# Attention weights left undivided: one reciprocal per visit, spread through DRAM and multiplied into the product with v

## The chip, the cores and the metric

One Trainium2 chip, one of its cores. The metric is the device time of one execution in microseconds (us). The engines are TensorE (PE in the profile; PEld is its loading of weights), VectorE (DVE), ScalarE (ACT), GpSimd (POOL) and SyncE (SP), which here issues every DMA. Each engine works through its own instructions in a fixed order and waits at an instruction whose inputs are not there.

## The reference

Attention with a threshold, then an expert layer. Batch 8, 8 heads, 576 queries and keys, 64 dimensions a head, inner width 2048, all in float32 (the expert weights arrive as float64).

```python
def _attn_ref(q, k, v, tau):
    scale = 1.0 / np.sqrt(q.shape[-1])
    scores = scale * np.matmul(q, k.transpose(0, 1, 3, 2))
    thresh = np.max(scores, axis=-1, keepdims=True) - tau
    scores = np.where(scores >= thresh, scores, -1000000000.0)
    scores = scores - np.max(scores, axis=-1, keepdims=True)
    attn = np.exp(scores)
    attn = attn / (np.sum(attn, axis=-1, keepdims=True) + 1e-09)
    return np.matmul(attn, v).astype(np.float32)

def _moe_ref(x, w_in, w_out):          # x: attention's output, [4608, 512]
    h = x @ w_in
    g = h * (1.0 / (1.0 + np.exp(-h)))
    return (g @ w_out).astype(np.float32)
```

## The kernel before

**Precision.** Products that need float32 run as several cheaper ones: a number is split into a high half (rounded) and a low half (the rest), and the product of the two low halves is left out. q and k are split for the scores, the attention weights w and v for the product with v, and its result x, the expert weights and the activation g for the experts.

**Visits and tiles.** A visit is a pair of heads (`VISITS`, L44). Batch 0 goes through four visits "low" and four "high"; "low" works in plain float32 (`direct`). The seven other batches have four visits "all" each: nine tiles of 128 queries by 576 keys, five of the first head (the fifth holds the last 64 queries of both heads) and four of the second. That is 288 tiles, 272 of them not direct. A tile's path:

- `scores` (L406): four matmuls, into one of two PSUM buffers s
- `soft1`: DVE takes the negated maximum (L416) and from it the threshold (L419)
- `soft1b`: ACT takes the exponential into w (L426), one of four buffers; its bias is the negated maximum
- `soft2`: DVE zeroes what is below the threshold and sums each row (L435), which frees s; then adds 1e-9 (L439) and takes the reciprocal (L443)
- `soft2b`: ACT scales w by that reciprocal (L448)
- `soft3`: the high half of w is rounded, by ACT in the first 36 slots (L457) and by POOL after them (L459); POOL subtracts for the low half in two pieces, 512 and 64 columns wide (L462, L465); a transposing DMA (L475) puts the halves, hl (three buffers), into wT (three buffers, one per head)

The hl row has nine blocks of 128: the high half takes four and a half of them, and the low half's last 64 columns lie in the fifth beside it, so that both meet the same rows of v there.

**Product with v.** `av` (L490) runs some tiles after a visit's last one: 14 steps for each of the two heads into the one PSUM bank a. `av_post` (L508, L509) writes x as two f16 halves, by ACT and DVE. `load_v`, `vmax`, `vscale` and `split_v` prepare v per batch; `vscale` holds a reduction across partitions on POOL (L113).

**Experts.** `h_unit` (L524) and its tanh, product and split (L532, L533, L541, L547), and `o_unit` (L562) with the store (L571, L573), are queued as units once a half batch of x is there, and laid between the tiles at a planned rate. After the last tile only such units are left.

**Order.** The text of the program is written slot by slot (L693 on), one tile per slot, with what is due in each (`at`) and priorities for scores and softmax. A scheduler with a model of the machine then fixes the order on each engine. SP's queue holds all the DMAs in one order.

## Time and profile before

| | |
|---|---|
| times of the three runs | 1360.35, 1365.4, 1726.3 us; median 1365.4 |
| profiled execution | 1360.35 us, span 1360.4 us |
| mean granted TensorE clock | 0.950 |
| PE busy | 1183.7 us, 87% of the span |
| DVE busy | 1002.8 us, 74% |
| ACT busy | 817.5 us, 60% |
| POOL busy | 789.9 us, 58% |
| DMA | 158.15 MB, mean 116 GB/s |

The span runs from the first to the last instruction of the profiled execution, which is also its time. A busy share is a mean over stages with different limits: until about 200 us the expert weights are decoded beside the first visits, up to about 1190 us attention and experts run together, and the rest is experts alone. Matmuls are pipelined, so a busy PE is not PE at its peak; the profile shows a mean of 287 ns for a matmul of L524, while 1312 matmuls end in the last 160 us, one per 122 ns. In the rows below, "x<-y" are a group's output and inputs by the names above, "xN" its count, then busy us, mean ns, and the idle time of the engine just before it with what ended it.

### The profile page before, as it was taken

What the parts mean: (1) busy time and instruction counts of PE and PEld (TensorE: products, weight loads), DVE (VectorE), ACT (ScalarE), POOL (GpSimd) and SP (SyncE); (2) the same over time, 40 slices, a digit from 0 to 9 for tenths busy, and PEclk for the clock granted to TensorE, in tenths of its full rate; (3) what the DMA queues carried; (4) which work ended last, traced back from release to release, by engine and by line L of the source; (5) the groups of instructions that cost most, each with busy time, mean ns of one, the idle gap of its engine ahead of it and who ended that gap; (6) DMA issues with size and microseconds to landing.
All of it is one profiled execution on the core that took longest, in us unless ns stands there. A gap on an engine that the chain in (4) does not pass through costs nothing.

```text
span 1360.4 us, 26858 instructions
## 1 busy us (share of the span) xinstructions
PE 1183.7 (87%) x9392; PEld 899.9 (66%) x9392; DVE 1002.8 (74%) x2619; ACT 817.5 (60%) x1493; POOL 789.9 (58%) x964
## 2 busy tenths in 40 slices
PE   3774787898599979898899969899799999999998
PEld 2453555666477757676677757677577777777777
DVE  4987997897598967968497856869478787872421
ACT  3776775675476756656375745757367666662432
POOL 2647984787478656754476646556467666661000
PEclk9887888999799999999899979999799999999999
DMA  6454955778467656664475556565466565543000
GB/s 226 140 185 125 197 129 94 146 139 170 88 133 155 122 106 129 131 128 86 99 132 124 118 96 136 101 127 121 82 122 116 115 129 115 106 88 53 6 19 18
DMA packets 363479, 158.15 MB, mean 116 GB/s; under 512 B 329552, under 2 KB 338256, under 8 KB 363344
## 3 DMA queue, kind: packets, MB, share of 16 engines
q1 hardware_dynamic: 363344, 156.43, 55.5%
q8 instruction: 74, 1.21, 0.4%
q14 instruction: 61, 0.50, 0.1%
HBM read 66.72 MB, written 9.44 MB: 56 GB/s over the span
## 4 chain that ended last, share of the span: by engine, by line
DVE 35%; PE 34%; issue 13%; ACT 6%; POOL 6%; DMA 5%; SPq 2%; POOLq 0%; ACTq 0%; DVEq 0%
PE o L562 15%; PE h L524 8%; DVE w L435 8%; DVE sm L416 6%; DVE gbuf L547 6%; PE s L406 5%; PE a L490 5%; DVE qstack L310 3%; DVE th L533 3%; DMA vraw<-in_vL 2%; DMA wT<-hl 2%; ACT w L426 2%; POOL hl L459 2%; POOL hl L462 2%; ACT w L448 2%
## 5 line engine op out<-in xcount | busy, mean ns | idle before, releaser
L524 PE MATMUL h<-x,wst 128*128 128x288 f16 (+2 forms) x3072 | 422.3, 290 | 22.6 <-DVE th L533 19.1
L562 PE MATMUL o<-gbuf,wst 128*128 128x288 f16 (+2 forms) x3072 | 419.4, 293 | 22.4 <-DVE gbuf L547 16.1
L562 PEld LDWEIGHTS <-wst 128*128 128x128 f16 x3072 | 296.4, 100 | 117.1 <-issue 27.1
L459 POOL TENSOR_SCALAR hl<-w 128x576 f16<-128x576 f32 x264 | 187.3, 710 | 317.9 <-ACT w L448 69.1
L524 PEld LDWEIGHTS <-wst 128*128 128x128 f16 x3072 | 290.7, 99 | 119.2 <-issue 37.5
L462 POOL TENSOR_TENSOR hl<-w,hl 128x512 f16<-128x512 f32 x272 | 332.0, 1220 | 28.0 <-issue 13.9
L426 ACT ACTIVATE w<-s,sm 128x576 f32<-128x576 f32 x288 | 211.0, 736 | 204.5 <-POOL hl L465 135.4
L435 DVE SCALAR_TENSOR_TENSOR w<-s,sm,w 128x576 f32<-128x576 f32 x288 | 232.6, 810 | 110.4 <-ACT w L426 108.7
L448 ACT ACTIVATE w<-w,sm 128x576 f32<-128x576 f32 x288 | 218.2, 770 | 86.5 <-DVE sm L443 81.6
L416 DVE TENSOR_REDUCE sm<-s 128x1 f32<-128x576 f32 x288 | 215.1, 748 | 44.4 <-PE s L406 42.3
L406 PE MATMUL s<-khi,qstack 128*128 128x288 f32 x608 | 160.4, 346 | 70.0 <-DVE w L435 36.9
L547 DVE SCALAR_TENSOR_TENSOR gbuf<-th,gbuf 128x288 f16<-128x288 f32 (+2 forms) x256 | 167.3, 656 | 20.9 <-ACT gbuf L541 20.2
L406 PEld LDWEIGHTS s<-khi,qstack 128*128 128x128 f32 x608 | 98.5, 198 | 98.8 <-issue 71.4
L490 PE MATMUL a<-wT,v 128*64 128x288 f16 (+1 forms) x1680 | 142.4, 294 | 16.1 <-DMA wT<-hl 15.0
L532 ACT ACTIVATE th<-h,msc 128x288 f32<-128x288 f32 (+2 forms) x256 | 126.3, 495 | 49.5 <-DVE gbuf L547 30.0
L541 ACT ACTIVATE gbuf<-th 128x288 f16<-128x288 f32 (+2 forms) x252 | 109.9, 438 | 44.5 <-DVE th L533 43.9
L406 PE MATMUL s<-klo,qstack 128*128 128x288 f32 x608 | 134.2, 304 | 0.0
L533 DVE SCALAR_TENSOR_TENSOR th<-th,h 128x288 f32<-128x288 f32 (+2 forms) x256 | 113.2, 444 | 27.6 <-ACT th L532 25.4
L490 PEld LDWEIGHTS <-v 128*64 128x64 f16 x1680 | 91.3, 110 | 56.7 <-issue 41.9
L465 POOL TENSOR_TENSOR hl<-w,hl 128x64 f16<-128x64 f32 x272 | 115.3, 424 | 0.0
L406 PEld LDWEIGHTS s<-klo,qstack 128*128 128x128 f32 x608 | 102.2, 197 | 0.0
L320 POOL TENSOR_TENSOR klo<-kraw,khi 128x576 fp32r<-128x576 f32 x64 | 95.6, 1493 | 1.4 <-ACT khi L318 1.3
(82 smaller groups left out, 868.8 us busy)
## 6 DMA issues: line engine op xcount, KB each, us to landing
qraw<-in_qT SPq DMA_DIRECT2D x128, 144.0 KB, 3.0
kraw<-in_kT SPq DMA_DIRECT2D x128, 144.0 KB, 3.0
vraw<-in_vL SPq DMA_DIRECT2D x32, 320.0 KB, 3.5
wraw<-in_w_out SPq DMA_DIRECT2D x16, 512.0 KB, 4.0
out_t<-ot SPq DMA_DIRECT2D x56, 144.0 KB, 2.0
wT<-hl SPq DMA_TRANSPOSE x304, 3.3
gbuf<-in_w_in SPq DMA_DIRECT2D x8, 512.0 KB, 5.1
wraw<-in_w_in SPq DMA_DIRECT2D x8, 512.0 KB, 4.9
```

Of the source, the lines that this page charges most:

```text
L406: nc.tensor.matmul(s_ps[:, j, :HALF], lhs, kk[:, j * HALF : (j + 1) * HALF], start=(n == 0), stop=(n == len(seq) - 1),)
L416: nc.vector.tensor_reduce(out=negm, in_=s_ps[:, :, :HALF], op=ALU.max, axis=AX.XY, negate=True)
L426: nc.scalar.activation(wtile[t].rearrange("p (j c) -> p j c", j=2), sps[t][:, :, :HALF], AF.Exp, bias=small[t][:, 0:1],)
L435: nc.vector.scalar_tensor_tensor(out=w3, in0=s_ps[:, :, :HALF], scalar=sm[:, 1:2], in1=w3, op0=ALU.is_ge, op1=ALU.mult, accum_out=sm[:, 2:3],)
L448: nc.scalar.activation(w, w, AF.Copy, scale=r)
L459: nc.gpsimd.tensor_scalar(out=fl[:, 0:S], in0=w, scalar1=1.0, scalar2=1.0, op0=ALU.mult, op1=ALU.mult)
L462: nc.gpsimd.tensor_tensor(out=fl[:, 640:1152], in0=w[:, 0:512], in1=fl[:, 0:512], op=ALU.subtract)
L490: nc.tensor.matmul(a_ps[odd * D : (odd + 1) * D, :n], vt[:, lo_v, odd, kv, :], wT[v, b * H + 2 * p + odd][:, kw, c0 - base : c0 - base + n ...
L524: nc.tensor.matmul(ph[:, :n], wi(c, f, lo_w), x16[b, lo_x][:, c, c0 : c0 + n], start=(k == 0), stop=(k == 11),)
L533: nc.vector.scalar_tensor_tensor(out=th[:, :n], in0=th[:, :n], scalar=1.0, in1=ph[:, :n], op0=ALU.add, op1=ALU.mult,)
L547: nc.vector.scalar_tensor_tensor(out=g[:, 1, :n], in0=th[:, :n], scalar=2.0**-14, in1=g[:, 0, :n], op0=ALU.mult, op1=ALU.subtract,)
L562: nc.tensor.matmul(ps[:, :n], wo(f, d, lo_w), g[:, lo_g, :n], start=(f == 0 and k == 0), stop=(f == NF - 1 and k == 2),)
```

## The change

The weights w are no longer divided by their sum. For every tile that is not direct:

- the threshold moves from DVE to POOL, and POOL also makes a bias for the exponential: the negated maximum plus 5 ln 2, so that w is 32 times larger and its halves keep enough bits undivided
- the sum of each row goes into one column of a visit's tile `sums`; L439, L443 and L448 fall away
- the high half is always ACT's; the low half is one subtraction of 576 columns on POOL, right behind the high one in hl
- once per visit, `spread_sums` takes one reciprocal of all tiles' sums (up to nine columns), writes it to DRAM as one row, and reads it back by three DMAs as `rows`, spread over the partitions of each head's columns
- `av_post` multiplies the product with v by `rows` on DVE into a float32 tile; ACT rounds its high half, POOL subtracts for the low one

The low half of w now begins in the middle of a block, so v's high half must be there in a second arrangement: `split_v` makes nine blocks, the last four by two DMAs within SBUF. The host puts v's first 64 rows where the doubled last 64 stood; the direct visits read the last 64 from `vlast`. To make room, w has three buffers instead of four, raw v four instead of five (so v is loaded twice from batch 1 on: once for its maximum, once to be split), and th, o and the new x share four buffers. The dates of v's work and of batch 0's splits move.

```diff
 def split_v(b, p):
-    o = sb.tile([P, 2, 2, 5, D], F16, tag="v16", name=f"v16_{b}_{p}", bufs=4)
-    nc.scalar.activation(o[:, 0], t, AF.Copy, scale=s)
+    hi = sb.tile([P, 2, 9, D], F16, tag="vhi", name=f"vhi_{b}_{p}", bufs=3)
+    lo = sb.tile([P, 2, 5, D], F16, tag="vlo", name=f"vlo_{b}_{p}", bufs=3)
+    nc.scalar.activation(hi[:, :, 0:5, :], t, AF.Copy, scale=s)
...
+    nc.sync.dma_start(out=hi[0:D, :, 5:9, :], in_=hi[D:P, :, 0:4, :])
+    nc.sync.dma_start(out=hi[D:P, :, 5:9, :], in_=hi[0:D, :, 1:5, :])
 def soft1(t):
-    w = sb.tile([P, S], F32, tag="w32", name=f"w32_{t}", bufs=4)
+    w = sb.tile([P, S], F32, tag="w32", name=f"w32_{t}", bufs=3)
...
-        nc.vector.tensor_scalar(
+        if tiles[t][0] not in direct:
+            nc.gpsimd.tensor_scalar(
+                out=sm[:, 5:6], in0=negm, scalar1=LIFT * math.log(2.0), scalar2=1.0,
+                op0=ALU.add, op1=ALU.mult,
+            )
+        (nc.vector if tiles[t][0] in direct else nc.gpsimd).tensor_scalar(
             out=thr, in0=negm, scalar1=-1.0, scalar2=ntau, op0=ALU.mult, op1=ALU.add
 def soft2(t):
+    total = sums[v][:, t - first_tile[v] : t - first_tile[v] + 1]
         op0=ALU.is_ge, op1=ALU.mult, accum_out=total,
+    if v not in direct:
+        small.pop(t)
+        return
+def spread_sums(v):
...
+    nc.vector.tensor_scalar(
+        out=r[:, :n], in0=sm[:, :n], scalar1=1e-9 * 2.0**LIFT, scalar2=None, op0=ALU.add
+    )
+    nc.vector.reciprocal(out=r[:, :n], in_=r[:, :n])
+    d = dram.tile([9 * P], F32, tag="rs", name=f"rs_{v}", bufs=4)
+    nc.sync.dma_start(out=d[: n * P].rearrange("(j p) -> p j", p=P), in_=r[:, :n])
+    R = sb.tile([P, S], F32, tag="rows", name=f"rows_{v}", bufs=2)
+    nc.sync.dma_start(out=R[0:D, :cols], in_=d[0:cols].partition_broadcast(D))
+    nc.sync.dma_start(
+        out=R[D:P, cols - D : cols], in_=d[cols : cols + D].partition_broadcast(D)
+    )
+    nc.sync.dma_start(
+        out=R[D:P, : cols - D], in_=d[cols + D : 2 * cols].partition_broadcast(D)
+    )
 def soft3(t):
-    if t < EARLY:
-        nc.scalar.activation(fl[:, 0:S], w, AF.Copy)
-    else:
-        nc.gpsimd.tensor_scalar(
-            out=fl[:, 0:S], in0=w, scalar1=1.0, scalar2=1.0, op0=ALU.mult, op1=ALU.mult
-        )
-    nc.gpsimd.tensor_tensor(
-        out=fl[:, 640:1152], in0=w[:, 0:512], in1=fl[:, 0:512], op=ALU.subtract
-    )
-    nc.gpsimd.tensor_tensor(
-        out=fl[:, 576:640], in0=w[:, 512:576], in1=fl[:, 512:576], op=ALU.subtract
-    )
+    nc.scalar.activation(fl[:, 0:S], w, AF.Copy)
+    nc.gpsimd.tensor_tensor(out=fl[:, S : 2 * S], in0=w, in1=fl[:, 0:S], op=ALU.subtract)
 def av(v, p, c0, n):
-    steps = [(0, k, k if k < 5 else k - 5) for k in range(9)] + [(1, k, k) for k in range(5)]
+    steps = [(vhi, k) for k in range(9)] + [(vlo, k) for k in range(5)]
 def av_post(v, p, c0, n, a_ps):
+    x = sb.tile([P, WID], F32, tag="th", name=f"x32_{v}_{c0}", bufs=4)
+    nc.vector.tensor_tensor(
+        out=x[:, :n], in0=a_ps[:, :n], in1=rows[v][:, c0 - base : c0 - base + n], op=ALU.mult
+    )
+    nc.scalar.activation(hi, x[:, :n], AF.Copy)
+    nc.gpsimd.tensor_tensor(out=lo, in0=x[:, :n], in1=hi, op=ALU.subtract)
 # schedule
+            if p == 0:
+                at(-2, load_vlast)
...
+        at(last_b + 1, lambda v=v: spread_sums(v))
...
-                at(V_SLOT + p, lambda p=p: split_v(0, p))
+                at(first_high + 5 * p - 2, lambda p=p: split_v(0, p))
...
-                at(u + 9 * p - 40, lambda b=b, p=p: load_v(b, p))
-                at(u + 9 * p - 34, lambda b=b, p=p: vmax(b, p))
-                at(u + 9 * p + 4, lambda b=b, p=p: split_v(b, p))
+                at(u + 6 * p - 36, lambda b=b, p=p: load_v(b, p))
+                at(u + 6 * p - 30, lambda b=b, p=p: vmax(b, p))
+                at(u + 9 * p - 2, lambda b=b, p=p: load_v(b, p))
+                at(u + 9 * p + 3, lambda b=b, p=p: split_v(b, p))
```

More of the change, by code (lines that the diff above doesn't have):

```diff
@@ L217, in wo, with load_vlast @@
         return w16[:, 4 * NK + f, o : o + P]
+    vlast = sb.tile([P, H, D], F32, tag="rows", name="vlast", bufs=2)
+    def load_vlast():
+        nc.sync.dma_start(out=vlast[D:P], in_=vL[0, 0:D, :, 4, :])
     vmx = {}
@@ L225, in load_v @@
     def load_v(b, p):
-        t = sb.tile([P, 2, 5, D], F32, tag="vraw", name=f"vraw_{b}_{p}", bufs=5)
+        t = sb.tile([P, 2, 5, D], F32, tag="vraw", name=f"vraw_{b}_{p}", bufs=4)
         nc.sync.dma_start(out=t, in_=vL[b, :, 2 * p : 2 * p + 2])
@@ L381, in attention_moe @@
     small = {}
+    sums = {}
+    rows = {}
+    first_tile = {}
     wT = {}
@@ L427, in soft1b @@
             wtile[t].rearrange("p (j c) -> p j c", j=2), sps[t][:, :, :HALF], AF.Exp,
-            bias=small[t][:, 0:1],
+            bias=small[t][:, 0:1] if tiles[t][0] in direct else small[t][:, 5:6],
         )
@@ L443, in soft2 @@
         nc.vector.reciprocal(out=sm[:, 4:5], in_=sm[:, 3:4])
+    def spread_sums(v):
+        kind = visits[v][2]
+        ta, tb, ranges = VISITS[kind]
+        n = len(ta) + len(tb)
+        cols = sum(c for _, c in ranges)
+        sm = sums.pop(v)
+        r = sb.tile([P, 9], F32, tag="rsum", name=f"rsum_{v}", bufs=2)
+        nc.vector.tensor_scalar(
[12 more added lines that the diff above has]
+        )
+        rows[v] = R
     def soft2b(t):
+        if tiles[t][0] not in direct:
+            return
         w = wtile[t]
@@ L502, in new_x16, with av_post @@
             x16[b, r] = xp[b % 2].tile([P, NK, S], F16, tag=f"x16_{r}", name=f"x16_{b}_{r}")
[L504 removed]
+    def av_post(v, p, c0, n, a_ps):
+        b = visits[v][0]
         if (b, 0) not in x16:
```

48 lines of the change are left out of this document (28 added, 20 removed).

## The prediction

> **What bounds the kernel now.** I read first how busy TensorE is by stage, then what it waits for, then what holds the engine that it waits for. The table by windows of the profile before has one row per stage (start:end, length, then busy us and instructions of PE, PEld, DVE, ACT and POOL, the granted clock, the DMA share, GB/s):
>
> ```profile
> 0.00:200.00 200.00, 127.41 (x761) 87.33 (x761) 168.44 (x397) 131.74 (x242) 130.91 (x138) 0.85 0.62 167
> 200.00:400.00 200.00, 163.64 (x1250) 121.87 (x1250) 159.23 (x427) 126.35 (x217) 136.98 (x171) 0.91 0.66 128
> 400.00:1000.00 600.00, 539.23 (x4410) 415.20 (x4410) 452.59 (x1219) 363.87 (x660) 364.25 (x461) 0.97 0.60 118
> 1000.00:1200.00 200.00, 196.75 (x1666) 152.25 (x1665) 164.42 (x441) 134.87 (x249) 134.32 (x165) 1.00 0.59 114
> 1200.00:1360.00 160.00, 156.62 (x1312) 123.21 (x1310) 58.12 (x138) 60.71 (x127) 23.40 (x33) 1.00 0.19 36
> sum 1360.00, PE 1183.66 PEld 899.87 DVE 1002.81 ACT 817.53 POOL 789.86; mean PE 236.73 PEld 179.97 DVE 200.56 ACT 163.51 POOL 157.97
> ```
>
> PE's work does not change, so only its idle time and its clock can. It idles 72.6 us of the first 200, 36.4 of the next 200, 60.8 of the 600 after them and 6.6 in the rest: 176 us. The clock is low exactly where PE idles (0.85, 0.91) and 1.00 where it doesn't, so idle time that goes also brings a little clock back. The second view is what PE waited for (total us, times, longest):
>
> ```profile
> PE s L406 <- DVE w L435: 36.9, 26, 10.6
> PE h L524 <- DVE th L533: 19.1, 20, 2.8
> PE o L562 <- DVE gbuf L547: 16.1, 6, 5.0
> PE a L490 <- DMA wT<-hl: 15.0, 5, 8.8
> ...
> POOL hl L459 <- issue: 67.5, 8, 11.1
> POOL v_all L113 <- issue: 43.9, 7, 7.5
> ```
>
> Most waits name DVE, but the last two rows point further back. Once per batch POOL runs a reduction across partitions (L113, for the scale of v), and around it POOL stands still for no visible reason. The timeline of batch 6 (start, length, idle before in brackets) shows what that does:
>
> ```profile
> 792.61 0.67 POOL L459 TENSOR_SCALAR hl<-w 128x576 f16<-128x576 f32 x1 [0.60 <-DMA wT<-hl]
> 799.61 0.38 POOL L113 PARTITION_ALL_REDUCE v_all<-v_one  x1 [6.33 <-issue]
> 807.15 1.14 POOL L462 TENSOR_TENSOR hl<-w,hl 128x512 f16<-128x512 f32 x1 [7.17 <-issue]
> ...
> 808.60 0.74 ACT L426 ACTIVATE w<-s,sm 128x576 f32<-128x576 f32 x1 [14.36 <-POOL hl L465]
> ...
> 803.06 0.82 PE L406 MATMUL s<-khi,qstack 128*128 128x288 f32 x2 [6.09 <-DVE sm L419]
> 810.35 0.82 PE L406 MATMUL s<-khi,qstack 128*128 128x288 f32 x2 [5.00 <-DVE sm L443]
> ...
> 220.40 0.50 PE L406 MATMUL s<-khi,qstack 128*128 128x288 f32 x2 [0.48 <-DVE v_sc L131]
> 968.58 0.82 PE L406 MATMUL s<-khi,qstack 128*128 128x288 f32 x2 [4.30 <-DVE sm L443]
> ```
>
> POOL is away from 793.3 to 807.2. DVE waits for the reduction's result in the first half, the exponentials wait in the second for POOL to free a buffer of weights, and PE idles 11.1 us. Such PE rows stand at six places after 200 us, 15 rows from 220.40 to 968.58, 54 us together. So of the 100.4 us idle between 200 and 1200, 54 belong to this pause and 46 are small waits, mostly for DVE.
>
> **The change, priced.** Rows by line and shape (us busy in all, mean ns):
>
> ```profile
> L419 DVE TENSOR_SCALAR sm<-sm,ntau 128x1 f32<-128x1 f32 x288 | 59.0, 207 | 2.8
> L439 DVE TENSOR_SCALAR sm<-sm 128x1 f32<-128x1 f32 x288 | 41.4, 145 | 1.2
> L443 DVE RECIPROCAL sm<-sm 128x1 f32<-128x1 f32 x288 | 44.2, 156 | 2.5
> L448 ACT ACTIVATE w<-w,sm 128x576 f32<-128x576 f32 x288 | 218.2, 770 | 86.5 <-DVE sm L443 81.6 <-DVE v_sc L131 4.3
> L457 ACT ACTIVATE hl<-w 128x576 f16<-128x576 f32 x8 | 5.4, 674 | 0.0
> L459 POOL TENSOR_SCALAR hl<-w 128x576 f16<-128x576 f32 x264 | 187.3, 710 | 317.9 <-ACT w L448 69.1 <-issue 67.5 <-DMA wT<-hl 58.7
> L462 POOL TENSOR_TENSOR hl<-w,hl 128x512 f16<-128x512 f32 x272 | 332.0, 1220 | 28.0 <-issue 13.9
> L465 POOL TENSOR_TENSOR hl<-w,hl 128x64 f16<-128x64 f32 x272 | 115.3, 424 | 0.0
> L543 POOL TENSOR_SCALAR gbuf<-th 128x256 f16<-128x256 f32 x4 | 1.7, 434 | 1.3 <-DVE th L533 1.0
> L768 POOL MEMSET const-float32-1.0<- 128x1 f32 x1 | 0.1, 99 | 0.0
> L509 DVE SCALAR_TENSOR_TENSOR x<-a,x 128x288 f16<-128x288 f32 x56 | 25.2, 449 | 43.9 <-ACT x L508 43.8
> ```
>
> DVE: 272 of the 288 tiles lose the threshold, the addition and the reciprocal, 272 x (207+145+156) = 138 us. The 32 visits gain an addition and a reciprocal of up to nine columns, 32 x 0.30 = 10 us by the same rows. The product with the spread reciprocals takes the place of L509 at about its 449 ns. Net -128 us.
>
> ACT: the scaling of the weights (770) goes and the rounding to f16 comes from POOL (674), -96 ns for most tiles, some -30 us; the 60 new roundings of x stand where L508 stood.
>
> POOL loses 187+332+115 = 635 us. Its new subtraction is one of 576 columns: (1220-424)/448 = 1.78 ns a column, so 1220+64x1.78 = 1334 ns, 272 times 363 us. The low half of x comes to POOL: 60 x 0.82 = 49 us. Threshold and bias come, 544 instructions of one column. No such row exists; between 99 (a MEMSET) and 434 (256 columns) I take 200, near DVE's 145 to 207: 109 us, with ends of 54 and 236. Net -114 (-169 to +13).
>
> SP and the DMA queue (issue ns min/median/max, then us to landing of a transpose, then KB and us to landing of a load of v):
>
> ```profile
> L475 SPq DMA_TRANSPOSE wT<-hl x304: 1199/1297/2433, 116.1 to 1238.4; - x152
> DMA to landing us min/median/max: 2.8/3.3/5.9
> L285 SPq DMA_DIRECT2D kraw<-in_kT x128: 465/582/1677, 68.0 to 1157.1; - x128
> vraw<-in_vL SPq DMA_DIRECT2D x32, 320.0 KB, 3.5
> ```
>
> The changed program issues 922 DMAs, the old 701: per visit one write of the sums and three reads back, two copies inside the high half of v, and a second load of v in seven batches. 221 x 0.58 = 128 us more of SP's time. The 272 tiles run from 116.1 to 1238.4 in the first of these rows, 4.13 us a tile and 37 us a visit of nine, of which SP issued 10 x 1.30 + 11 x 0.58 = 19; now 23. The write must land (about 3 us, between the row of v and that of the transposes) before the reads can be issued, and SP stands meanwhile. What that holds up is seen in SP's order. In visit 19, before:
>
> ```order
> L286 DMA qraw_21_35_8247<-in_qT 64x576 [waits DMAHW2_49]
> L475 DMA_TRANSPOSE wT_19_31_7595<-hl_152_7590 128x9x64 [waits DMAHW3_49,PE_49]
> L475 DMA_TRANSPOSE wT_19_31_7595<-hl_153_7649 128x9x128 [waits DMAHW4_49]
> L475 DMA_TRANSPOSE wT_19_31_7595<-hl_154_7702 128x9x128 [waits DMAHW5_49]
> L227 DMA vraw_5_3_9144<-in_vL 128x640 [waits DMAHW6_49,DVE_49]
> ```
>
> and in the same visit now, where rs is the write of the reciprocals and rows their way back:
>
> ```order
> L296 DMA qraw_21_35_8140<-in_qT 64x576 [waits DMAHW3_49]
> L487 DMA rs_19_7708<-rsum_19_7705 128x9x1 [waits DMAHW4_49,DVE_49]
> L489 DMA rows_19_7710<-rs_19_7708 64x576 [waits DMAHW5_49,DMAHW4_49]
> L490 DMA rows_19_7710<-rs_19_7708 64x64 [waits DMAHW6_49]
> L493 DMA rows_19_7710<-rs_19_7708 64x512 [waits DMAHW7_49]
> L520 DMA_TRANSPOSE wT_19_31_7503<-hl_152_7499 128x9x64 [waits DMAHW0_49,PE_49]
> L520 DMA_TRANSPOSE wT_19_31_7503<-hl_153_7553 128x9x128 [waits DMAHW1_49]
> ```
>
> Three transposes now stand behind the trip. But the first of them waits for PE anyway (its buffer, until the product of the visit before), so I price the trip at 0, hidden by that wait. Without the cover it costs up to 4 us a visit.
>
> The threshold's move adds a hop to the softmax: POOL stands between the maximum and the exponential. Around the pause of batch 5, POOL before:
>
> ```order
> L459 TENSOR_SCALAR hl_158_7899<-w32_158_7837 128x576 [waits DMAHW7_49,Activation_49]
> L113 ISA
> L113 ISA v5_all_9802<-v5_one_9800 128x1 [waits DVE_49]
> L459 ISA
> L459 TENSOR_SCALAR hl_159_7981<-w32_159_7889 128x576 [waits DMAHW0_49,Activation_49]
> L462 TENSOR_TENSOR hl_158_7899<-w32_158_7837,hl_158_7899 128x512 [waits Pool_49]
> ```
>
> and now (sm is a tile's column of maximum, threshold and bias):
>
> ```order
> L438 TENSOR_SCALAR sm_141_6758<-sm_141_6758,ntau_83 128x1
> L113 ISA
> L113 ISA v5_all_9672<-v5_one_9670 128x1 [waits DVE_49]
> L512 ISA
> L512 TENSOR_TENSOR hl_140_6769<-w32_140_6710,hl_140_6769 128x576 [waits DMAHW5_49,Activation_49,Pool_49]
> L512 TENSOR_TENSOR hl_141_6832<-w32_141_6759,hl_141_6832 128x576 [waits DMAHW5_49,Activation_49]
> L434 TENSOR_SCALAR sm_142_6817<-sm_142_6817 128x1 [waits DVE_49]
> ```
>
> The bias of tile 142 stands behind the pause and two subtractions, so its exponential comes 2 x 1.33 + 0.2 us after POOL is back. Before, it came 1.45 us after (807.15 to 808.60). In three later batches the bias stands first and comes sooner. I price the pause at 0, with +10 at worst (seven times 1.4).
>
> The sum, against the profiled execution's 1360.4 us: the 46 us of small waits after 200 us lose a third, since DVE loses 128 of 1003 us and POOL a seventh of its load: -15 (0 to -30). In the first 200 us DVE is busy 168; 20 tiles there lose 0.51 us each, -10, of which I count -8 (0 to -15). Batch 0's second products now follow each other through the single PSUM bank, DVE's product and new transposes: +6 (0 to 15). Clock with the idle time: -2. Weights, loads of v, vlast and the copies of v: 0, since each lands some tiles ahead of its use; bare, a load costs its 3.5 us. Together -19: 1341. The median of the runs, 1365.4, lies 5 above the profiled execution; the forecast goes half of the way: 1343.
>
> One rule of the Trainium skill (SBUF — State Buffer, "Who interferes with whom") speaks against putting the bias on GpSimd: a VectorE instruction with two inputs in SBUF and a GpSimd instruction that reads SBUF exclude each other, the later one waiting until the other ends. The trace agrees; one input of L533 lies in PSUM, both of L547 in SBUF (ns min/median/max):
>
> ```profile
> L533 DVE SCALAR_TENSOR_TENSOR th<-th,h x256: 396/445/490, 123.1 to 1333.7; 128x288 f32<-128x288 f32 x112, 128x256 f32<-128x256 f32 x8, 128x320 f32<-128x320 f32 x8
> L547 DVE SCALAR_TENSOR_TENSOR gbuf<-th,gbuf x256: 408/459/1682, 128.3 to 1334.7; 128x288 f16<-128x288 f32 x112, 128x256 f16<-128x256 f32 x8, 128x320 f16<-128x320 f32 x8
> ```
>
> By the rule a bias can wait out a gbuf, and DVE's gbuf meets fewer POOL instructions than before; an estimate from these rows is +0.1 us a tile, inside the slack of rival two, so the sum stays.
>
> **Rivals.** One, DVE's relief counts fully: in the stretches where the experts' first products run, DVE has both softmax and th/gbuf, and most of the 46 and of the first 200 us' DVE waits go. -35, -20, clock -5 makes 1300; with the +6 for batch 0 and half of the 5 us to the median 1309, and up to 1325 if the gain is smaller by a quarter: say 1315. For it: the waits name DVE. Against it: PE is busy 98% from 1000 to 1200 with DVE at 82%.
>
> Two, on the other side: the softmax becomes the bound through POOL. POOL's order after is bias, bias, subtraction, subtraction, by pairs of tiles, and the next bias stands behind the second subtraction:
>
> ```profile
> L426 ACT ACTIVATE w<-s,sm 128x576 f32<-128x576 f32 x288 | 211.0, 736 | 204.5 <-POOL hl L465 135.4 <-DVE sm L416 35.4 <-DVE sm L439 22.1
> L435 DVE SCALAR_TENSOR_TENSOR w<-s,sm,w 128x576 f32<-128x576 f32 x288 | 232.6, 810 | 110.4 <-ACT w L426 108.7
> ```
>
> A pair then takes 2 x 0.74 (exponentials) + 0.81 + 0.67 (rounding) + 1.33 + 0.4 = 4.7 us, against 8.3 us that a pair takes now (2 x 4.13). It decides once waits at the hops pass 3.6 us a pair; from there 0.3 us more costs the 126 pairs of the 28 full visits 38 us: 1381, and with 0.5 us 1406. For it: ACT's and DVE's orders put the experts' work between the hops. Against it: ACT is busy 61% from 400 to 1000, POOL 61%, so a hop rarely waits long.
>
> Three: the trip of the sums isn't covered, and PE waits for the late transposes: 1 of the 4 us in each of 28 visits is 28 us, 1371. For it: SP stands at every trip. Against it: PE waited for transposes only 15.0 us in all. Four: what DVE saves is slack, since PE's static order and the pauses decide, and the times stay: 1355 to 1368.
>
> **Chances.** Forecast (1328 to 1354) 0.36, rival one 0.25, two 0.16, three 0.09, four 0.14. A measurement of this kernel tells about 2% from no change, so the limits are 1333 and 1388. Faster: rival one and a third of the forecast, 0.37. Slower: two thirds of rival two and a quarter of three, 0.13, and 0.07 taken from four for costs with no row in the trace: 0.20. Same 0.43. The range 1308 to 1396 leaves out the ends of rivals one and two. The forecast's own range is 1328 to 1354.
>
> **What would show it.** Right: DVE near 865 us busy, POOL near 675, ACT near 790; the one-column POOL instruction near 0.2 us; PE idle near 155 us, still some 54 of it at the pauses; no large wait of PE for wT. Wrong: PE's scores waiting for w with the exponential waiting for POOL's sm (rival two), PE's a waiting for wT behind SP's L489 (rival three), or PE's idle after 200 us under 70 (rival one).

## The result: 20% slower

The changed kernel takes 1631.49 us (median of four runs, 1630.61 to 1637.27), the kernel before 1362.88 (four runs, 1354.11 to 1726.3): a ratio of 1.2005, 95% interval 1.1961 to 1.205. The forecast was 1343 with a range of 1308 to 1396, so it was wrong in direction and far outside its range. The run of 1726.3 lies far above the other three and is left out of the ratio. The profiled execution took 1632.1 us, span 1630.0, with a mean granted clock of 0.879 (0.950 before).

The table by windows after the change, with the columns of the prediction's first table:

```profile
0.00:200.00 200.00, 110.20 (x636) 77.50 (x636) 142.56 (x309) 107.76 (x202) 109.16 (x124) 0.83 0.62 164
200.00:400.00 200.00, 141.16 (x987) 105.08 (x987) 114.75 (x217) 98.37 (x165) 104.09 (x143) 0.82 0.65 114
400.00:1000.00 600.00, 463.73 (x3619) 352.62 (x3618) 357.90 (x701) 304.08 (x558) 288.79 (x427) 0.89 0.63 118
1000.00:1200.00 200.00, 149.45 (x1158) 114.35 (x1159) 108.61 (x216) 97.44 (x180) 88.74 (x131) 0.86 0.54 109
1200.00:1400.00 200.00, 167.30 (x1326) 127.74 (x1325) 126.72 (x242) 110.22 (x206) 98.66 (x144) 0.91 0.55 107
1400.00:1630.00 230.00, 204.89 (x1672) 160.05 (x1670) 86.88 (x184) 87.64 (x176) 44.90 (x66) 0.95 0.25 47
sum 1630.00, PE 1236.73 PEld 937.33 DVE 937.41 ACT 805.50 POOL 734.34; mean PE 206.12 PEld 156.22 DVE 156.24 ACT 134.25 POOL 122.39
```

PE now idles 393.3 us, 216.6 more than before, in every stage in which attention runs: 136.3 of the 600 us from 400 on, where it was 60.8. Its busy time is 53.0 us longer for the same 9392 matmuls, in stages whose clock fell to 0.82 to 0.91. Both together are the 269.6 us between the spans. No engine is busier as a share of the span than before, so none became the bound by its load. The page's shares of the chain of work that ended last, by engine and line, name the place:

```profile
PE 30%; DMA 27%; DVE 15%; issue 12%; POOL 8%; ACT 5%; SPq 3%; POOLq 0%; DVEq 0%; ACTq 0%
```

DMAs hold 27% of the chain, where it was 5%; the same section gives 11% of the span to the write rs and 11% to the transposes. The waits (us in all, times, longest):

```profile
POOL hl L512 <- ACT hl L511: 391.4, 169, 11.8
ACT hl L511 <- DMA wT<-hl: 265.7, 75, 12.0
ACT w L445 <- POOL sm L434: 210.3, 144, 12.4
DVE w L460 <- ACT w L445: 206.6, 97, 12.5
PE s L420 <- DVE w L460: 164.2, 38, 20.3
...
PE a L535 <- DMA wT<-hl: 20.2, 6, 8.3
```

Read from the fifth row up: PE's scores wait for DVE, DVE for the exponential, the exponential for POOL's bias, POOL, at its subtraction, for ACT's high half, and ACT for transposes to free a buffer hl. The first wait in which no engine is named is ACT's for the transposes, so the next view is the waits of SP, which issues them, and that of the DMAs (KB each, median us from issue to landing):

```profile
SPq L489 <- DMA rs<-rsum: 242.3, 30, 10.5
```

```profile
wT<-hl SPq DMA_TRANSPOSE x304, 3.4
...
rows<-rs SPq DMA_DIRECT2D x28, 144.0 KB, 3.0
rows<-rs SPq DMA_DIRECT2D x28, 128.0 KB, 3.2
...
rs<-rsum SPq DMA_DIRECT2D x28, 4.5 KB, 9.8
```

The write of a visit's reciprocals, 4.5 KB, the smallest transfer of the visit, takes 9.8 us to land (9.8 to 11.3 as medians of the four kernels that write it so), where a load of 320 KB of v took 3.5. SP stands behind it at the first read back, 30 times, 242.3 us in all. The timeline of one visit (start, length, idle before in brackets):

```profile
1032.91 0.40 SPq L487 DMA_DIRECT2D rs<-rsum  x1
1043.36 0.46 SPq L489 DMA_DIRECT2D rows<-rs  x1
1043.91 6.62 SPq L520 DMA_TRANSPOSE wT<-hl  x4
...
1036.34 0.50 ACT L587 ACTIVATE th<-h,msc 128x288 f32<-128x288 f32 x1
1047.18 0.68 ACT L511 ACTIVATE hl<-w 128x576 f16<-128x576 f32 x1 [10.34 <-DMA wT<-hl]
...
1038.52 3.11 PE L579 MATMUL h<-x,wst 128*128 128x288 f16 x24
1050.98 1.36 PE L617 MATMUL o<-gbuf,wst 128*128 128x288 f16 x5 [9.35 <-DVE th L588]
```

From 1032.9 to 1043.4 SP issues nothing. The transposes that stood behind the trip start at 1043.9, ACT gets its buffer at 1047.2, and as ACT's instructions stand in one order, its work for the experts waits behind the rounding of w too: PE runs dry at 1041.6 and goes on at 1051.0.

### The profile page after: what moved, and what is told of

It is laid out like the page before. It is cut to its first block, busy times and chain, and to the rows that moved or that the text cites. A ratio compares the mean times of both kernels' runs of the same rounds, so it can differ in the third digit from the quotient of the medians.

```text
span 1630.0 us, 26738 instructions
## 1 busy us (share of the span) xinstructions
PE 1236.7 (76%) x9392; PEld 937.3 (58%) x9392; DVE 937.4 (58%) x1867; ACT 805.5 (49%) x1485; POOL 734.3 (45%) x1032
## 4 chain that ended last, share of the span: by engine, by line
PE 30%; DMA 27%; DVE 15%; issue 12%; POOL 8%; ACT 5%; SPq 3%; POOLq 0%; DVEq 0%; ACTq 0%
PE o L617 14%; DMA rs<-rsum 11%; DMA wT<-hl 11%; PE h L579 7%; PE s L420 4%; POOL hl L512 4%; PE a L535 4%; DVE w L460 3%; DVE sm L430 2%; DVE gbuf L602 2%; ACT hl L511 2%; DVE th L588 2%; ACT w L445 1%; POOL klo L330 1%; DMA wraw<-in_w_out 1%
## 5 line engine op out<-in xcount | busy, mean ns | idle before, releaser
L512 POOL TENSOR_TENSOR hl<-w,hl 128x576 f16<-128x576 f32 x272 | 355.9, 1314 | 410.8 <-ACT hl L511 391.4
L579 PE MATMUL h<-x,wst 128*128 128x288 f16 (+2 forms) x3072 | 435.7, 297 | 51.9 <-DVE th L588 48.8
L460 DVE SCALAR_TENSOR_TENSOR w<-s,sm,w 128x576 f32<-128x576 f32 x288 | 232.8, 813 | 211.4 <-ACT w L445 206.6
L511 ACT ACTIVATE hl<-w 128x576 f16<-128x576 f32 x272 | 184.9, 681 | 301.4 <-DMA wT<-hl 265.7
L445 ACT ACTIVATE w<-s,sm 128x576 f32<-128x576 f32 x288 | 210.9, 737 | 219.2 <-POOL sm L434 210.3
L420 PE MATMUL s<-khi,qstack 128*128 128x288 f32 x608 | 172.0, 368 | 164.6 <-DVE w L460 164.2
L535 PE MATMUL a<-wT,vhi 128*64 128x288 f16 (+1 forms) x1080 | 110.0, 318 | 66.6 <-DVE x L563 39.5
L420 PE MATMUL s<-klo,qstack 128*128 128x288 f32 x608 | 143.3, 321 | 0.0
L434 POOL TENSOR_SCALAR sm<-sm 128x1 f32<-128x1 f32 x272 | 79.8, 293 | 135.4 <-DVE sm L430 103.5
L596 ACT ACTIVATE gbuf<-th 128x288 f16<-128x288 f32 (+2 forms) x252 | 109.0, 438 | 51.7 <-DVE th L588 50.9
L535 PEld LDWEIGHTS <-vhi 128*64 128x64 f16 x1080 | 64.6, 118 | 102.7 <-issue 64.1
L420 PEld LDWEIGHTS s<-klo,qstack 128*128 128x128 f32 x608 | 111.1, 214 | 0.0
L567 POOL TENSOR_TENSOR x<-x,x 128x288 f16<-128x288 f32 (+1 forms) x60 | 47.5, 791 | 124.1 <-ACT x L566 124.1
```

Of the source, the lines that this page charges most:

```text
L420: nc.tensor.matmul(s_ps[:, j, :HALF], lhs, kk[:, j * HALF : (j + 1) * HALF], start=(n == 0), stop=(n == len(seq) - 1),)
L445: nc.scalar.activation(wtile[t].rearrange("p (j c) -> p j c", j=2), sps[t][:, :, :HALF], AF.Exp, bias=small[t][:, 0:1] if tiles[t][0] in d ...
L460: nc.vector.scalar_tensor_tensor(out=w3, in0=s_ps[:, :, :HALF], scalar=sm[:, 1:2], in1=w3, op0=ALU.is_ge, op1=ALU.mult, accum_out=total,)
L511: nc.scalar.activation(fl[:, 0:S], w, AF.Copy)
L512: nc.gpsimd.tensor_tensor(out=fl[:, S : 2 * S], in0=w, in1=fl[:, 0:S], op=ALU.subtract)
L535: nc.tensor.matmul(a_ps[odd * D : (odd + 1) * D, :n], vt[:, odd, kw, :], wT[v, b * H + 2 * p + odd][:, kw, c0 - base : c0 - base + n], sta ...
```

## The experiments

Each time is the median of its runs, beside runs of the kernel before on the same chip (1361 to 1365 us). "Changed" is the changed kernel. The scheduler fixes the order of every kernel anew, so an edit also moves instructions that it doesn't touch. The large differences below are tied to the edit by the landing times and stands that were measured with them; one of a few us can be the order's as well as the edit's.

### Is it the trip, and what of it?

**no_trip.** One constant tile in place of the trip:

```diff
+    ones_rows = const.tile([P, S], F32, name="ones_rows")
+    nc.vector.memset(ones_rows, 2.0**-14)
...
-        d = dram.tile([9 * P], F32, tag="rs", name=f"rs_{v}", bufs=4)
-        nc.sync.dma_start(out=d[: n * P].rearrange("(j p) -> p j", p=P), in_=r[:, :n])
...
+        R = ones_rows
```

> The changed kernel without the trip of the sums: the write of the reciprocals and the three reads back are left out, and the product with v is multiplied by a constant row of 2^-14 instead, so the weights' sums are not divided out of the output. Theory A (SP stands after each write of the reciprocals until it has landed, 242 us in 30 stands, and the transposes behind it come late): 1330 to 1370 us. Theory B (the softmax is bound by its hop through POOL): the hop is still there, 1550 to 1630. Theory C (the small packets of the trip slow all other transfers): as A, 1330 to 1370.

Measured: 1384.27 us, 1.0131 of before (1.0086 to 1.0176). 247 us of the change's 269 are the trip's. But the rest is no gain either: the kernel that has all of the relief and no trip is 19 us slower than the kernel before, and lies 14 above the range of theories A and C. Theory B alone is out.

**stale_rows.** The reads take what the visit before wrote:

```diff
+        drams[v], d = d, drams[v - 1] if v - 1 in drams and visits[v - 1][2] == kind else d
         R = sb.tile([P, S], F32, tag="rows", name=f"rows_{v}", bufs=2)
```

> All four DMAs of the trip stay, but each visit reads back what the visit before it wrote, so no read waits for a write that has just been issued. The output is divided by the sums of the visit before and scaled by 2^-9. A: SP no longer stands, 1335 to 1385 us. B: 1550 to 1630. C: the packets are all there, 1500 to 1630.

Measured: 1607.3 us, 1.1768 (1.1718 to 1.1819). Theory A missed by over 200 us, and C's number came. The timeline of this kernel says why:

```profile
1032.35 0.38 SPq L489 DMA_DIRECT2D rs<-rsum  x1
1033.00 4.07 SPq L523 DMA_TRANSPOSE wT<-hl  x3
1043.18 0.46 SPq L492 DMA_DIRECT2D rows<-rs  x1
...
1036.62 0.44 ACT L599 ACTIVATE gbuf<-th 128x288 f16<-128x288 f32 x1 [0.32 <-DVE th L591]
1045.09 0.68 ACT L514 ACTIVATE hl<-w 128x576 f16<-128x576 f32 x1 [8.02 <-DMA wT<-hl]
```

The transposes are issued right behind the write, at 1033.0, and still ACT waits until 1045.1 for the first of them: 12.1 us where 3.5 is the median. So the transposes land late also when SP issues them in time. The DMA view of this kernel from 1032 to 1048 us shows how (busy tenths of the 16 engines and GB/s in 40 slices of 0.4 us):

```profile
DMA  0006739829999999999999995999900079700000
GB/s 0 0 0 5 6 74 152 129 35 220 183 20 19 20 16 24 42 48 20 34 28 83 30 15 9 58 51 67 90 0 7 9 174 330 265 20 0 0 0 0
```

The bytes of the transposes begin to move at about 1034, right behind the packets of the write. But from 1036.4 to 1043.6 the engines are shown busy nearly all the time at 9 to 90 GB/s. SP's read, which waits for the write to land, is issued at 1043.2, and behind it the rate goes up to 330. So it is not only the news of their landing that is late: the transposes' own packets are slow while the write is on its way, which is what theory C said, for the transfers behind the write. SP stood as well, 100.7 us in 16 stands, since the reads for the next visit had moved up to four transposes behind their own write, and found it still on its way: the edit took away less of the wait than I had claimed (it also puts a factor of 2^9 into the reciprocals). The Trainium skill (DMA: Bandwidth & Descriptors, "Queues, rings and completion order") states that the increment of a DMA's semaphore lands only after every earlier write of the same DMA engine; the 12.1 us agree with it, but that rule says nothing of slow packets.

**before_plus_trip.** The trip as dead work in the kernel before (the short tile is what fits there):

```diff
+        nc.sync.dma_start(out=d[: n * P].rearrange("(j p) -> p j", p=P), in_=r[:, :n])
+        R = sb.tile([P, 160], F32, tag="rows", name=f"rows_{v}", bufs=1)
+        nc.sync.dma_start(out=R[0:D, :cols], in_=d[0:cols].partition_broadcast(D))
```

> The kernel before with the trip added as dead work: the sums of a visit are gathered in nine columns, one addition and one reciprocal, the write to DRAM with pieces of 4 bytes, and three broadcast reads (160, 64 and 96 columns, which are not used); weights are divided as before. A: 1540 to 1640 us. B: no hop on POOL here, 1355 to 1380. C: 1450 to 1640.

Measured: 1620.22 us, 1.1864 (1.1813 to 1.1914), with SP standing behind the write 261.8 us. The trip costs 255 us in a kernel whose softmax has no hop. So it is the trip, in either kernel.

### Why the write takes so long

The sums lie as 128 partitions of nine; in DRAM they are wanted as nine rows of 128, so each of the 1152 numbers is a piece of its own.

**row_wise_write.** The same bytes, 128 pieces of 36:

```diff
-        nc.sync.dma_start(out=d[: n * P].rearrange("(j p) -> p j", p=P), in_=r[:, :n])
+        nc.sync.dma_start(out=d[: n * P].rearrange("(p j) -> p j", p=P), in_=r[:, :n])
```

> The changed kernel with the reciprocals written in the order in which they lie in SBUF: 128 pieces of 36 bytes instead of 1152 of 4, same bytes, same place in the program, same three reads. The rows then come back in another order, so each query is divided by another one's sum (and scaled by 2^-9). In stale_rows a transpose issued 0.7 us behind the write landed after 12.1 us instead of 3.4, so the write itself holds up the queue. Theory D (the write's landing time goes by its number of pieces, 1152 in about 8.7 us): it lands in about 3 us and the kernel takes 1385 to 1425 us, near no_trip's 1384. Theory E (any write to DRAM that is read back at once costs this): 1560 to 1640.

Measured: 1419.86 us, 1.0398 (1.0366 to 1.043). 212 us go with another order of the numbers in DRAM (a factor of 2^9 goes into an instruction that is there anyway). Until the fourth of these writes the order of every engine is the same in both kernels; SP issues that write at 240.3 us here and at 250.1 in changed, though the first one came 1.9 us earlier there. Behind it the orders differ in places. In this kernel's DMAs and SP's waits:

```profile
rs<-rsum SPq DMA_DIRECT2D x28, 4.5 KB, 1.9
```

```profile
SPq L489 <- DMA rs<-rsum: 31.0, 23, 2.6
```

**three_by_three_write.** 384 pieces of 12 bytes:

```diff
+        k = 3 if n == 9 else 5
+        nc.sync.dma_start(
+            out=d[: n * P].rearrange("(g p k) -> p g k", p=P, k=k),
+            in_=r[:, :n].rearrange("p (g k) -> p g k", k=k),
+        )
```

> row_wise_write with pieces of 12 bytes in the full visits (384 pieces of three reciprocals; batch 0's four visits write rows of 20 bytes). Rows come back in another order, as there. Theory D in proportion: the write lands 9.8 us after its issue with 1152 pieces and 1.9 with 128, so 3.9 us with 384, and of the 211 us between the two kernels a quarter comes back: 1420 + 53 = 1473 us (1450 to 1495). If only pieces of 4 bytes are slow: 1412 to 1432. If any piece below some size is as slow as a whole 4-byte one in bytes moved (same bytes, same time): 1600 to 1640.

Measured: 1452.83 us, 1.0658 (1.0614 to 1.0701), the write landing after 3.4 us, SP standing 61.3 us. It lies between the two as the number of pieces does, a little under proportion, and neither of the other readings fits. Theory E is out, and the division into pieces sets the landing time. Whether it does so by the number of pieces, as theory D has it, or by their length isn't separated: at 4.5 KB the one goes down as the other goes up. Batch 0's writes in changed, 640 pieces of 4 bytes, took 9.4 us, nearly as long as the 1152 of 4 bytes. The three side by side:

| kernel | pieces | landing us | SP's stands us | above no_trip us |
|---|---|---|---|---|
| changed | 1152 | 9.8 | 242.3 | 247 |
| three_by_three_write | 384 | 3.4 | 61.3 | 69 |
| row_wise_write | 128 | 1.9 | 31.0 | 36 |

In these three, what the kernel loses is close to what SP stands. It is no rule: stale_rows lies 223 us above no_trip with stands of 100.7, since there the transposes stood right behind the write and were late themselves.

The Trainium skill (DMA: Bandwidth & Descriptors, "Anatomy of one DMA") gives 2.0 us plus the bytes at 436 GB/s for a DMA on GpSimd's path, an estimate of 2.0 us here. The row-wise write, issued by SP, agrees (1.9); the piece-wise one takes five times that, for which the formula has no term.

**row_write_no_reads.** no_trip with the row-wise write alone:

```diff
+        d = dram.tile([9 * P], F32, tag="rs", name=f"rs_{v}", bufs=4)
+        nc.sync.dma_start(out=d[: n * P].rearrange("(p j) -> p j", p=P), in_=r[:, :n])
         R = ones_rows
```

> no_trip (1384 us) with the row-wise write of the reciprocals added, 128 pieces, and no reads back; x is still multiplied by the constant. Between no_trip and row_wise_write (1420) lie 36 us. If they are the write's: 1410 to 1422. If they are the three reads' (SP stands about 2 us until the write has landed, then issues three DMAs, and the transposes behind them come later): 1382 to 1394.

Measured: 1392.87 us, 1.023 (1.0178 to 1.0283). Of the last 36 us some 9 are the write's, 27 the three reads' with the stand before them.

**turned_write.** Complete: TensorE turns the reciprocals, so that DRAM gets nine pieces of 512 bytes.

```diff
+        tp = ps_a.tile([P, 512], F32, tag="a", name=f"tp_{v}")
+        nc.tensor.matmul(tp[:n, :P], r[:, :n], ident, start=True, stop=True)
+        rT = R[:9, :P]
+        nc.vector.tensor_copy(rT[:n], tp[:n, :P])
+        nc.sync.dma_start(out=d[: n * P].rearrange("(j p) -> j p", p=P), in_=rT[:n])
```

> The changed kernel, complete, with the 128x9 reciprocals turned by TensorE (one product with a unit matrix into the bank of the products with v, one small copy on VectorE), so that the write to DRAM has 9 pieces of 512 bytes. D: lands in 2 to 3 us, 1380 to 1425 us. E: 1560 to 1640.

Measured: 1431.89 us, 1.0492 (1.0471 to 1.0512), just above the bound given. SP stands 17.0 us. Against the row-wise order, which no complete kernel can use, the one product, the copy and the shared bank come to 12 us, with what the order of instructions adds.

### The softmax's hop through POOL

**hop_on_dve** (from changed), **no_trip_hop_on_dve** (from no_trip), **turned_write_hop_on_dve** (from turned_write), the same edit in each:

```diff
-            nc.gpsimd.tensor_scalar(
+            nc.vector.tensor_scalar(
                 out=sm[:, 5:6], in0=negm, scalar1=LIFT * math.log(2.0), scalar2=1.0,
...
-        (nc.vector if tiles[t][0] in direct else nc.gpsimd).tensor_scalar(
+        nc.vector.tensor_scalar(
             out=thr, in0=negm, scalar1=-1.0, scalar2=ntau, op0=ALU.mult, op1=ALU.add
```

> Threshold and bias of the softmax on VectorE again, all else as changed (544 instructions of one column move from POOL to DVE). A: 1600 to 1640 us, as the changed kernel. B: 1350 to 1450. C: 1600 to 1640.

> no_trip (1384 us) with threshold and bias on VectorE. It asks what the 19 us are that no_trip lies above the kernel before. If the hop of the softmax through POOL: 1335 to 1368. If other parts (one weight buffer less, batch 0's late products, the second loads of v, the copies): 1378 to 1400.

> turned_write with threshold and bias on VectorE. D and the hop as second cause: 1340 to 1380 us, the version that could be as fast as the kernel before. D and other second causes: 1380 to 1425. E: 1560 to 1650.

Measured: 1649.74 (1.2083, 1.2012 to 1.2153), 1377.45 (1.0098, 1.0076 to 1.0119) and 1416.14 (1.0375, 1.0353 to 1.0396). With the trip in place the hop's return brings nothing (the intervals of 1.2083 and 1.2005 meet, and 1649.74 lies above all that was expected). Without the trip it brings 7 us, but the intervals overlap (1.0086 to 1.0176 against 1.0076 to 1.0119); in turned_write 16, clear of them. It is a second cause, small, and not all of no_trip's 19 us.

**before_threshold_on_pool.** In the kernel before, the threshold alone:

```diff
-        nc.vector.tensor_scalar(
+        (nc.vector if tiles[t][0] in direct else nc.gpsimd).tensor_scalar(
             out=thr, in0=negm, scalar1=-1.0, scalar2=ntau, op0=ALU.mult, op1=ALU.add
         )
```

> The kernel before with only the threshold of the softmax on POOL (272 instructions of 0.2 us less on VectorE, 56 us; the exponential does not wait for it). If relief of VectorE is worth what the forecast's sum gave it (a third of the small waits for 128 us): -5 to -10, 1354 to 1362. If it counts fully (rival one): 1335 to 1350. If POOL comes late with it, at the pauses above all: 1370 to 1390.

Measured: 1395.87 us, 1.0235 (1.0197 to 1.0273), above the highest range given. 56 us less of VectorE's instructions, and 33 us slower. The waits of this kernel:

```profile
DVE w L435 <- POOL sm L419: 113.0, 74, 9.0
POOL sm L419 <- DVE sm L416: 107.9, 56, 4.7
PE s L406 <- DVE w L435: 105.5, 40, 13.6
```

The exponential doesn't wait for the threshold, but the step behind it does: DVE waits 113.0 us for POOL, longest 9.0, and PE waits for that step 105.5 instead of 36.9. A one-column instruction on POOL (358 ns in the mean here) stands behind whatever POOL's order has before it. This is the mechanism of rival two, in the kernel before.

### Where the relief went

**before_light_dve.** The kernel before with two small VectorE instructions fewer in each of the 272 tiles:

```diff
+        if tiles[t][0] in direct:
+            nc.vector.tensor_scalar(
+                out=thr, in0=negm, scalar1=-1.0, scalar2=ntau, op0=ALU.mult, op1=ALU.add
...
-            in0=s_ps[:, :, :HALF], scalar=sm[:, 1:2], in1=w3,
+            in0=s_ps[:, :, :HALF], scalar=sm[:, 1:2] if tiles[t][0] in direct else low, in1=w3,
...
-        nc.vector.reciprocal(out=sm[:, 4:5], in_=sm[:, 3:4])
+        nc.vector.reciprocal(out=sm[:, 4:5], in_=total)
```

> The kernel before without two small VectorE instructions in each of its 272 tiles: the threshold (207 ns; a constant of -1e30 takes its place, so every weight is kept) and the addition and scaling of the sum (145 ns; the output comes out 2^-12 as large in those columns). VectorE does 96 us less, nothing is added to any engine. If the forecast's sum was right for VectorE (-23 us for 128 us): about -17, 1342 to 1352. If the relief counts fully (rival one): 1310 to 1335. If it is slack (rival four): 1355 to 1370.

Measured: 1356.15 us against 1361.02, 0.9958 (0.9944 to 0.9973): 4.9 us for 96 us of instructions, a real but small gain, at the lower edge of what rival four gave and a third of what the forecast's rate gave. PE's idle time in the profile is 171.8 us (span 1355.8 less 1184.0 busy), 176.7 before. So PE's waits for DVE were, for the most part, not waits for DVE to have time. POOL's relief alone was not tried.

**no_trip_own_rings, no_trip_rings_and_hop, rings_hop_four_weights, rings_hop_four_weights_loads.** What else keeps no_trip above the kernel before? Step by step: th, x and the output tile get buffers of their own; hop on DVE as well; a fourth buffer of weights; v's first loads as before.

```diff
-        x = sb.tile([P, WID], F32, tag="th", name=f"x32_{v}_{c0}", bufs=4)
+        x = sb.tile([P, WID], F32, tag="x32", name=f"x32_{v}_{c0}", bufs=1)
...
-        w = sb.tile([P, S], F32, tag="w32", name=f"w32_{t}", bufs=3)
+        w = sb.tile([P, S], F32, tag="w32", name=f"w32_{t}", bufs=4)
...
-                at(u + 6 * p - 36, lambda b=b, p=p: load_v(b, p))
+                at(u + 9 * p - 40, lambda b=b, p=p: load_v(b, p))
```

> no_trip (1384 us) with the four buffers that th, the scaled product x and the output tile share in turn given out as two for th, one for x, one for the output. In no_trip batch 0's first scaled product stood at 219 us on VectorE although its product with v was done at 147, behind an output tile that took the buffer before it; there the kernel falls 25 us behind the kernel before by 450 us, and gains 8 after. If the shared ring is the cause: batch 0's products are early again, 1352 to 1370. If it is not, or single buffers cost as much: 1378 to 1395.

> no_trip with own buffers for th, x and output, and threshold and bias on VectorE. If ring and hop are what is left besides the trip, and add up: 1345 to 1366. If the ring does nothing at the end: 1374 to 1380, as no_trip_hop_on_dve (1377).

> The kernel of no_trip_rings_and_hop with four buffers of weights instead of three (the constant is a single column here, which frees the space). If three buffers hold the softmax back: 10 us or more below that kernel, 1340 to 1366. If not: within 5 us of it.

> As rings_hop_four_weights, and the first loads of v and their maxima at the tiles where the kernel before has them (nine tiles apart, from 40 ahead). If the earlier pauses of POOL at the start (batch 1's at 78 us instead of 100) cost the 15 us by which the changed schedule is late at its first product of the experts: 8 us or more below that kernel. If not: within 5 us.

Measured: 1381.79 (1.0138, 1.0098 to 1.0178), 1371.42 (1.0063, 1.0038 to 1.0088), 1378.75 (1.0119, 1.007 to 1.0168) and 1368.51 (1.0033, 1.0002 to 1.0063). The ring moved batch 0's first scaled product from 218.9 to 157.9 us and the 193rd matmul of the experts' first product from 232.8 to 197.0, as expected, and the end by 2: what came early waited later. (The reason that the expectation gives isn't shown: in no_trip the output tile it names starts at 219.3, behind x.) With the hop gone it is worth 6, with intervals that overlap. A fourth buffer of weights gives nothing (7 us the wrong way, also with intervals that overlap), the loads 10 on top of it. With everything put back that the runs found, and without any trip, the kernel is as fast as the one before, within 0.6%. What this last kernel keeps of the relief is mostly POOL's (589.8 us busy for 789.9, while DVE has 984.2 for 1002.8, as the hop went back to it). That relief, less what the change still adds, is worth nothing here that could be measured.

**turned_write_own_rings, best_complete.** The complete kernel with these: hop on DVE and own buffers; then v's first loads as well.

> turned_write_hop_on_dve (1416 us), complete, with the same own buffers for th, x and the output. Ring theory: 1385 to 1402. Otherwise 1410 to 1425. Not under 1365 in either case, unless the trip's rest (row_wise_write lies 36 us above no_trip) came from the shared ring too.

> turned_write_own_rings (1406 us), complete, with the first loads of v at the times of the kernel before. The loads were worth 10 us in rings_hop_four_weights_loads: 1390 to 1400. If that gain depended on the fourth buffer of weights: 1402 to 1410. Above the kernel before in either case, since the three reads back cost 27 us and the turning and the write some 15 more.

Measured: 1405.6 (1.0312, 1.0263 to 1.0362) and 1408.47 (1.0351, 1.0325 to 1.0376). The loads' 10 us don't come here, as the second reading had it; the rings' 10 us or so put the first kernel between its two ranges. Of the 269 us, 226 could be won back in a complete kernel; no complete version beats the kernel before.

## Why the prediction was wrong, step by step

**The step that failed** is the price of the trip: "The write must land (about 3 us, between the row of v and that of the transposes)", and from it "so I price the trip at 0, hidden by that wait. Without the cover it costs up to 4 us a visit". The write takes 9.8 us. The rows that I took it from were transfers of hundreds of KB in long pieces; the nearest in size isn't the nearest in kind, and the pieces, 9 x 128 of 4 bytes, stood in the diff's rearrangement. The cover was a second error: the first transpose may wait for PE in the order, but SP's stand begins when the sums are there, and lasted 8.1 us a time (242.3 / 30) on top of what was hidden. And the transposes behind it are held up even where they are issued in time (12.1 us instead of 3.5 in stale_rows).

**Rival three was the right place at a ninth of the price.** It named the trip not covered and the transposes late, at 1 us in each of 28 visits; it was some 8 to 9 (247 / 28 = 8.8). It had 0.09 of the chance, and the range ended at 1396 by other cases. Its mark was named wrongly too: "PE's a waiting for wT" is 20.2 us, 15.0 before. The late transposes reached PE through the three buffers hl, ACT's order and the softmax, and so the chain of waits ends on DVE, as before. What came in its place was rival two's sign, the exponential waiting for POOL's bias (210.3 us), although hop_on_dve shows that the hop is not what costs the time there: a named wait tells where the delay passes, not where it starts.

**The gains of the sum didn't come.** It counted "the 46 us of small waits after 200 us lose a third" and -8 in the first 200. In no_trip PE's idle time from 400 to 1000 is 61.8 us (60.8 before), and in the first 200 84.8 (72.6). Its rows:

```profile
0.00:200.00 200.00, 115.17 (x657) 80.48 (x658) 154.23 (x331) 114.75 (x213) 122.94 (x136) 0.83 0.62 169
200.00:400.00 200.00, 158.81 (x1214) 118.68 (x1213) 141.89 (x267) 120.50 (x209) 120.70 (x177) 0.91 0.70 142
400.00:1000.00 600.00, 538.23 (x4400) 415.25 (x4399) 421.50 (x832) 361.35 (x670) 339.45 (x500) 0.95 0.64 129
1000.00:1200.00 200.00, 193.74 (x1621) 149.52 (x1619) 152.11 (x293) 130.35 (x246) 118.18 (x173) 1.00 0.68 125
```

before_light_dve measures the rate: 4.9 us for 96, a twentieth, where the sum took 23 for 128. Rival four, that DVE's saving is slack, is right but for those few us; rival one is out.

**Batch 0** was given +6 (0 to 15). PE idles 17.1 us more than before in no_trip's first two stages. The shared ring alone is not the cause (2 us at the end); hop, ring and loads together are 16. How these divide is not settled, since they depend on each other (the loads are worth 10 beside a fourth weight buffer, nothing in best_complete).

**Rival two**: the hop costs up to 16 us where the trip is short, 33 for the threshold alone in the kernel before. The mechanism was right, but the slack that it was given ("It decides once waits at the hops pass 3.6 us a pair") was too generous, and the sum had no term for the hop beside the pause's 0.

**Loads of the engines.** ACT 805.5 us (about 790 forecast) was nearly right. POOL 734.3 instead of 675: the subtraction is 1314 ns (1334 forecast), but one column costs 293 and 333 in the mean, not 200, so 544 of them are 170 us and not 109. Half of the bias instructions take no more than 191 ns (first row below: least, median, most), so the 200 was right for a bias that isn't held up. What it lacked are the waits of the others:

```profile
L434 POOL TENSOR_SCALAR sm<-sm x272: 180/191/808, 100.9 to 1483.3; 128x1 f32<-128x1 f32 x136
1113.98 1.57 DVE L320 SCALAR_TENSOR_TENSOR qstack<-qraw,gate,qstack 64x576 fp32r<-64x576 f32 x1
1114.91 0.69 POOL L434 TENSOR_SCALAR sm<-sm 128x1 f32<-128x1 f32 x1
```

The bias in the third row starts while DVE works on two inputs in SBUF (second row), and ends 0.05 us behind that, at 1115.60. Of the 82 bias instructions that started inside such an instruction of DVE, 79 took over 250 ns and ended about 50 ns behind it; of the 107 that started inside another one of DVE, with at most one input in SBUF, a single one took so long. The trace agrees with the Trainium skill's rule on who interferes with whom (SBUF — State Buffer), weighed in the prediction. Above their medians (191 and 264 ns), bias and threshold lose 47 us together, 0.17 us a tile where the prediction's estimate was 0.1. DVE 937.4 instead of 865:

```profile
L512 POOL TENSOR_TENSOR hl<-w,hl 128x576 f16<-128x576 f32 x272 | 355.9, 1314 | 410.8 <-ACT hl L511 391.4 <-issue 14.0 <-DMA wT<-hl 2.7
L438 POOL TENSOR_SCALAR sm<-sm,ntau 128x1 f32<-128x1 f32 x272 | 90.7, 333 | 0.0
L434 POOL TENSOR_SCALAR sm<-sm 128x1 f32<-128x1 f32 x272 | 79.8, 293 | 135.4 <-DVE sm L430 103.5 <-issue 21.1 <-DVE rsum L485 5.2
```

DVE's small instructions overlap their neighbours: in before_light_dve, instructions of 96 us in all took 57.6 us off its busy time (1002.8 to 945.2). A sum of durations overstates what their removal frees.

**The pauses** stayed, as forecast: POOL's idle time before L113 is 50.9 us in seven (43.9 before). Weights at three buffers showed no cost, as priced.

## What to carry to other kernels

Before a transfer to DRAM is priced, look at its contiguous pieces, how many and how short, and not only at its bytes: turning a 128x9 block on the way out made 4.5 KB the slowest transfer of the visit here. Where one queue issues everything, a DMA that is read back at once stops all that stands behind it, and one in many short pieces delays also what is issued behind it in time; so such a trip needs slack of its own length on that queue, not on the engine that uses its result. An engine that is most often named in the waits of a kernel whose orders are static need not be its bound: take a known amount off it alone, as in before_light_dve, before a change is built on its relief.

## What the runs showed of the hardware that was not expected

- The packets of the piece-wise write are over long before it lands. The DMA view of the changed kernel from 1033 to 1043 us (busy tenths of the 16 engines in 40 slices of 0.25 us):

```profile
DMA  0004771000000000000000000000020000000000
...
DMA packets 1174, 0.03 MB, mean 3 GB/s; under 512 B 1170, under 2 KB 1170, under 8 KB 1173
...
rs<-rsum SPq DMA_DIRECT2D x1, 4.5 KB, 10.4
```

  All packets fall between 0.75 and 1.75 us; the landing comes at 1043.3, and in the 8.5 us between the DMA engines are shown idle but for one slice, at 1040.3. What goes on there the records don't show. From the medians it is 7.7 ns a piece between 128 and 1152 pieces, but 5.9 up to 384 and 8.3 beyond. Batch 0's four writes of 640 pieces of 4 bytes took 9.4 us, nearly as long as 1152, so the number alone doesn't give the time. Other traffic is no plain reason: the two of them behind 200 us, where the DMAs move 114 GB/s, took 9.4 and 9.2.
- Transposes issued behind the write are slow themselves: 9 to 90 GB/s for some 7 us in stale_rows.
- A one-column instruction takes 191 or 264 ns on POOL in the median (bias, threshold), 145 to 207 on DVE. On POOL the mean is 293 to 358, as those that start while DVE has two inputs in SBUF end only behind it.
- Where the reads back stand right behind the write, the kernel loses about what SP stands (242.3 for 247, 61.3 for 69, 31.0 for 36 us).
